# Projecting queries and keys of an attention kernel by Strassen's scheme: seven products of block sums in place of eight block products

## The chip, the cores and the metric

One Trainium2 chip, of which the kernel uses one core. The metric is the device time of one execution in microseconds (us), lower is better. Every time below comes from timed runs or from one profiled execution of the kernel. TensorE does the matrix products (PE in the profile; its weight loads, which overlap them, are PEld), VectorE is DVE, ScalarE is ACT, GpSimd is POOL, and SyncE, which issues most transfers, is SP.

## The reference

Two attentions over the same 2048 rows of 512 numbers, mixed by a gate. Side A is softmax attention of 32 heads over all 2048 keys. Side B is attention in four segments of 512 with a causal mask, plus a linear memory of the earlier segments.

```python
def _A_ref(x, wqkv, wo):
    qkv = (x @ wqkv).reshape(B, S, 3, H, Dh).transpose(2, 0, 3, 1, 4)
    q, k, v = qkv[0], qkv[1], qkv[2]
    p = softmax(einsum("bhqd,bhkd->bhqk", q, k) * Dh ** -0.5)
    return einsum("bhqk,bhkd->bhqd", p, v) ... @ wo
g = sigmoid((x * gate_w).sum(-1, keepdims=True))
return g * _A_ref(x, A_wqkv, A_wo) + (1 - g) * _B_ref(x, B_wq, B_wk, B_wv, B_wo, B_beta)
```

Here S = 2048, D = 512, H = 32, Dh = 16; all is float32. What the change touches is `x @ wqkv` for the queries and keys of side A.

## The kernel before

The rows of x are worked in four chunks of 512 (`CH`). Every matrix operand is split into a high half, rounded to the type float32r, and the low half that is left over; a product is then three products: high by low, low by high, high by high. So a tile of 128 outputs by 512 rows of x, with the 512 inputs in four steps of 128, is 12 matmuls.

The program has a projection stage, and a main loop behind it. In the projection stage first come the projections of side A ("all keys"): queries of chunks 0 and 1, keys and values of all four chunks. The queries of chunks 2 and 3 (`LATER`) are made in the main loop. Then come the projections of side B, its memory, and the first 96 steps of the search for the row maxima. The main loop does scores, exponentials, products with the values and the output projection.

The stage runs in slots. A slot (`slot`, L360) is 12 matmuls in four places of three; behind each place it calls whatever was posted there: `post(n, place, f)` counts from the current slot, `post_at` names the slot. Each engine executes in the order in which the code is written, so this decides what stands behind what in the queues.

A tile of queries or keys (`qk_tile`, L418) goes to a bank of `pr_ps` (two banks). A slot later ScalarE copies the bank to `full` (L433) and casts it to the high half `q1` (L434), VectorE subtracts for the low half `q2` (L441), and SyncE stores both (L430); `q1` and `q2` have three buffers each. Tiles of values (`v_tiles`, L470) are copied to `vs` by ScalarE (L481) and stored once for a chunk; `vs` has one buffer. Operands are loaded into raw buffers and split by ScalarE and VectorE (L403, L404). The first four tiles of queries (`first_tiles`, L456) are made side by side in four banks, so that the product can begin with the first 128 rows of the weights.

GpSimd writes, by twenty small transfers (L378), rows of ones into the tiles in which the main loop will hold keys (`kA`, `kB`), and makes minima for side B's feature map (L438). Other banks in the stage: `me_ps` (two, tag "me") and `me_sm` (four, tag "sm"), used by side B's memory and the maxima.

Of the kernel before, what the change touches and what calls it, by code (L numbers as in the profile page):

```python
# [19 lines left out]
D = 512  # L20
# [27 lines left out]
def gated_mix(ctx, tc, x, xT, wqkv, a_wo, b_wq, b_wk, b_wv, b_wo, beta, gate_w, out):  # L48
# [284 lines left out]
    with ExitStack() as p0:  # L333
# [15 lines left out]
        ones = wk1.tile([128, CH], F32, tag="dn", name="ones")[0:2]  # L349
# [10 lines left out]
        def slot(ps=None, l=None, r=None):  # L360

            terms = [(a, b, k) for k in range(KT) for a, b in ((1, 0), (0, 1), (0, 0))]
            for place in range(4):
                if ps is not None:
                    for n in range(3 * place, 3 * place + 3):
                        a, b, k = terms[n]
                        nc.tensor.matmul(ps, l(a, k), r(b, k), start=(n == 0), stop=(n == 11))  # L367
                for f in posted.pop((now[0], place), []):
                    f()
            now[0] += 1  # L370

# [4 lines left out]
        for i, t in enumerate(kbuf["A"] + kbuf["B"]):  # L376
            for r in range(2):
                post_at(6 + i, 1 + 2 * r, lambda t=t, r=r: nc.gpsimd.dma_start(  # L378
                    raw(t)[64 * r + 48:64 * r + 50], ones.unsqueeze(1).broadcast_to([2, 2, CH])))

        def halves(pool, tag, src, load_slot, split_slot, tiles=None, queue=nc.sync):
# [3 lines left out]
            def load(i):  # L385
                t = tiles[i] if tiles else None
# [11 lines left out]
            def split(k):  # L398
# [5 lines left out]
                nc.vector.tensor_sub(hold[1][:, k], w, hold[0][:, k].bitcast(F32))  # L404
# [13 lines left out]
        def qk_tile(side, w, xc, o, dst, then=None, ps=None, n0=0):  # L418

            if ps is None:  # L420
                ps = pr_ps.tile([128, CH], F32, tag="pr", name="pr")
                slot(ps, lambda a, k: w[a][:, k, o * 128:(o + 1) * 128], lambda b, k: xc[b][:, k, :])
# [5 lines left out]
            def store(i, t):  # L428
                to = dst[16 * i:16 * i + 16].rearrange("d h t -> (d h) t") if side == "A" else dst[i].rearrange("h d t -> (h d) t")
                nc.sync.dma_start(to, raw(t))  # L430
# [21 lines left out]
            post(n0, 0, e0)  # L452
            post(n0, 1, e1)
            post(n0 + 1, 1, e2)

        def first_tiles(w, xc):  # L456

            banks = [(pr_ps if o < 2 else me_ps).tile([128, CH], F32, tag="pr" if o < 2 else "me", name="pr") for o in range(NO)]
            for k in range(KT):
                for i, (a, b) in enumerate(((0, 0), (0, 1), (1, 0))):  # L460
# [3 lines left out]
                    for f in [f for place in ((0,), (1,), (2, 3))[i] for f in posted.pop((now[0], place), [])]:  # L464
                        f()
# [713 lines left out]
```

## Time and profile before

| what | value |
|---|---|
| median of 3 runs | 1751.49 us (1750.65 to 1752.21) |
| the profiled execution | 1749.92 us |
| its span, first to last instruction | 1748.2 us |
| granted TensorE clock, mean | 1.000 |
| projections of side A | 5.7 us to about 115 us |
| first score of the main loop | 284.69 us |

The page gives, for each engine, its busy time, share of the span and count of instructions, and then 40 equal slices of the span with the busy share of each in tenths. The chain of waits is followed back from the last instruction, at each step to what released it. A group row has line, engine, operation, output and inputs with shapes, count, then busy time and mean ns of one, and behind the second bar the engine's idle time just before these instructions with what ended it. A row of a timeline has start and duration in us. A merged row with "x2" lasts from the first start to the last end. In a table of stretches each engine's busy time is followed by its count; the last three numbers are the granted clock, the share in which the transfer engines were busy, and GB/s.

### The profile page before, as it was taken

The page shows a single profiled execution, that of the slowest core. Times are in us where ns is not written, and L with a number is a line of the kernel's source. Part 1 is how long each engine was busy: PE and PEld are TensorE (multiplying, and loading weights), DVE is VectorE, ACT ScalarE, POOL GpSimd, SP SyncE. Part 2 cuts the span into 40 slices and gives each one's busy share as a digit, 9 for nine tenths or more (in the row PEclk, how much of TensorE's full clock was granted, in tenths as well). Part 3 has the DMA queues.
Part 4 walks back from the last instruction along what each step waited for, and adds up shares of the span by engine and source line. Part 5 has one row for each costly group of instructions (what it writes and reads, how often), then busy time and mean ns, then how long its engine had stood idle before and what let it go on. Part 6 is the DMA issues. An engine that isn't in the chain of part 4 may idle for free.

```text
span 1748.2 us, 41466 instructions
## 1 busy us (share of the span) xinstructions
PE 1741.4 (100%) x15229; PEld 890.4 (51%) x15229; DVE 1558.4 (89%) x3283; ACT 1434.5 (82%) x2751; POOL 696.7 (40%) x954
## 2 busy tenths in 40 slices
PE   9999999999999999999999999999999999999999
PEld 7887775444444444444444444444444444444444
DVE  4337778999999999999999999999999999999931
ACT  5455556888889898888888888888888888888884
POOL 3012233324262427353534353444344353535443
PEclk9999999999999999999999999999999999999999
DMA  7677667435453446444545454444444444444542
GB/s 251 220 245 244 209 214 205 120 103 149 120 152 102 130 127 196 125 143 132 147 122 150 123 142 136 134 139 127 148 126 153 127 132 118 148 118 146 150 153 63
DMA packets 149115, 261.61 MB, mean 150 GB/s; under 512 B 38793, under 2 KB 61353, under 8 KB 148401
## 3 DMA queue, kind: packets, MB, share of 16 engines
q1 hardware_dynamic: 146464, 254.42, 48.8%
q0 software_dynamic: 2304, 4.29, 1.0%
q8 instruction: 121, 1.98, 0.5%
q14 instruction: 82, 0.66, 0.1%
q10 hardware_dynamic: 144, 0.26, 0.1%
HBM read 174.39 MB, written 83.25 MB: 147 GB/s over the span
## 4 chain that ended last, share of the span: by engine, by line
PE 99%; ACT 0%; DMA 0%; issue 0%; DVE 0%; ACTq 0%
PE ops L155 40%; PE st L815 27%; PE sm L242 14%; PE pr L367 13%; PE sm L155 2%; PE pr L462 1%; PE mt_ps L232 0%; PE tps L601 0%; PE sm L815 0%; DMA raw<-xT 0%; PE mps L615 0%; ACT p L838 0%; PE num L574 0%; PE den L578 0%; PE ops L1121 0%
## 5 line engine op out<-in xcount | busy, mean ns | idle before, releaser
L838 ACT ACTIVATE p<-st 128x512 f32<-128x512 f32 x2261 | 1190.9, 601 | 146.8 <-PE sm L242 93.5
L275 DVE TENSOR_REDUCE pm<-sm 128x1 f32<-128x512 f32 x2048 | 1276.1, 682 | 10.3 <-PE sm L242 8.9
L242 PE MATMUL sm<-kA,qA 48*128 48x512 f32 x2048 | 661.3, 424 | 0.0
L815 PE MATMUL st<-qA,kA 50*128 50x512 f32 x2014 | 656.3, 432 | 0.0
L155 PE MATMUL ops<-p,vA 128*17 128x256 f32 (+3 forms) x6360 | 552.7, 445 | 0.2 <-ACT p L838 0.2
L815 PEld LDWEIGHTS st<-qA,kA 50*128 50x128 f32 x2014 | 327.0, 185 | 423.0 <-ACT p L838 382.2
L242 PEld LDWEIGHTS sm<-kA,qA 48*128 48x128 f32 x2048 | 337.5, 185 | 11.4 <-DVE ph L450 4.6
L939 POOL TENSOR_TENSOR rcp<-rec,minus 128x32 f32<-128x32 f32 x43 | 234.8, 5461 | 82.9 <-DMA rec<-dend 76.9
L290 DVE CUSTOM_DVE_ANT_0 rest<-sm,mask 128x128 f32<-128x128 f32 (+3 forms) x512 | 246.4, 481 | 0.4 <-PE sm L242 0.4
L155 PEld LDWEIGHTS ops<-p,vA 128*17 128x17 f32 x6360 | 129.3, 96 | 214.8 <-issue 183.4
L819 POOL TENSOR_SCALAR_AFFINE_SELECT p<-p 128x512 f32<-128x512 f32 x128 | 79.4, 637 | 265.9 <-ACT p L838 261.4
L242 PE MATMUL sm<-kB,qB 48*128 48x128 f32 (+3 forms) x512 | 166.1, 385 | 0.0
L815 PE MATMUL st<-qB,kB 50*128 50x512 f32 (+1 forms) x495 | 105.5, 329 | 0.3 <-ACT mt L235 0.3
L441 DVE TENSOR_TENSOR q<-full,q 128x512 fp32r<-128x512 f32 x56 | 38.8, 694 | 74.1 <-ACT q L434 69.6
L815 PEld LDWEIGHTS st<-qB,kB 50*128 50x128 f32 x495 | 68.6, 186 | 62.1 <-ACT p L838 50.4
L155 PE MATMUL ops<-p,vB 128*17 128x128 f32 (+3 forms) x1504 | 88.3, 350 | 0.0
L242 PEld LDWEIGHTS sm<-kB,qB 48*128 48x128 f32 x512 | 80.0, 184 | 0.0
L214 POOL TENSOR_TENSOR dm<-pm 128x32 f32<-128x32 f32 x32 | 7.9, 247 | 165.6 <-DVE pm L275 165.6
L438 POOL TENSOR_SCALAR mn<-full 128x512 f32<-128x512 f32 x24 | 36.9, 1536 | 88.0 <-ACT full L433 88.0
L433 ACT COPY full<-pr 128x512 f32<-128x512 f32 x56 | 32.7, 584 | 37.9 <-PE pr L367 32.7
L223 POOL CAST ms<-pm 128x16 fp32r<-128x16 f32 x32 | 6.3, 196 | 126.5 <-DVE pm L290 126.4
L955 POOL TENSOR_TENSOR v<-v,inv 128x512 f32<-128x512 f32 x31 | 39.8, 1284 | 27.4 <-DMA inv<-rdA 23.6
(203 smaller groups left out, 1618.7 us busy)
## 6 DMA issues: line engine op xcount, KB each, us to landing
kA<-kdA SPq DMA_DIRECT2D x256, 128.0 KB
vA<-vdA SPq DMA_DIRECT2D x31, 544.0 KB
kA<-kdA SPq DMA_DIRECT2D x256, 64.0 KB
qB<-qdB SPq DMA_DIRECT2D x192, 64.0 KB
kB<-kdB SPq DMA_DIRECT2D x192, 64.0 KB
kdA<-q SPq DMA_DIRECT2D x32, 256.0 KB
qdB<-q SPq DMA_DIRECT2D x32, 256.0 KB
qA<-qdA SPq DMA_DIRECT2D x64, 128.0 KB
```

Source lines behind the costliest of these rows:

```text
L155: behind[0] = nc.tensor.matmul(*args, **kw)
L242: nc.tensor.matmul(ps[:, n0:n0 + n], rows(qt[u][:, :, s * 128:(s + 1) * 128], h, 48), rows(k[:, :, k0:k0 + n], h, 48), start=True, stop=True)
L275: nc.vector.tensor_reduce(pm[:, h, s, kc:kc + 1], ps, axis=AX.X, op=ALU.max, negate=True)
L290: nc.vector.tensor_tensor_reduce(out=tri["rest"][:, 0:w], in0=ps[:, n0:n0 + w], in1=tri["mask"][:, CH - w:], scale=-1.0, scalar=3.0e38, op ...
L367: nc.tensor.matmul(ps, l(a, k), r(b, k), start=(n == 0), stop=(n == 11))
L438: nc.gpsimd.tensor_scalar_min(ph["mn"], full, 0.0)
L441: nc.vector.tensor_sub(q2, full, q1.bitcast(F32))
L815: nc.tensor.matmul(ps[:, n0:n0 + CH - q0], rows(k[:, :, b * 128:(b + 1) * 128], h, 50), rows(q[:, :, q0:], h, 50), start=True, stop=True)
L819: nc.gpsimd.affine_select(out=x, in_=x, pattern=[[0, 4], [1, 128]], base=0, channel_multiplier=-1, compare_op=ALU.is_ge, fill=0.0)
L838: nc.scalar.activation(p[:, h], ps, AF.Exp, scale=SCALE)
L939: eng.tensor_tensor(r, rec, minus, op=ALU.pow)
L955: eng.tensor_mul(k["v"], k["v"], k["inv"])
```

## The change

Queries and keys of side A are now projected for two chunks at a time. Weights and the two chunks of x are cut into two by two blocks: 256 inputs, 256 outputs, and one chunk of 512 rows each. Strassen's scheme in Winograd's form makes the four output blocks from seven block products of sums of blocks; a block product is, for each of two tiles of 128 outputs, 6 matmuls of the old shape. A pair of chunks is thus 14 products of 6 matmuls (`pair_tiles`), with two products in a slot, and takes 7 slots. It is done three times: queries of chunks 0 and 1, keys of 0 and 1, keys of 2 and 3. Values stay plain; they come first (chunks 0 and 1) and between the two key pairs (chunks 2 and 3). The stage of side A has 37 slots in place of 40.

The sums of x (`s_sums`) are made once for a pair of chunks, in the raw buffers, and the sums of the weights (`t_sum`) as well; each sum is then split into halves like every operand. VectorE and GpSimd share these. The split sums lie in the key tiles of the main loop (`kbuf`) and in its query buffers, so the rows of ones are now written at slot 38 and later. The products' banks are read by VectorE: adds join the seven products (`sums`, `out_tile`), two with a sum kept in SBUF each, and an output tile is an add out of a bank into `full` where it was a copy by ScalarE. Low halves are subtracted by VectorE or, for half of the tiles of the first key pair, by GpSimd.

```diff
-        def slot(ps=None, l=None, r=None):
+        PARTS = (1, 0), (0, 1), (0, 0)
+        def slot(products=()):
...
+        def pair_tiles(w, ts, xs, ss, cs, dst, eng_):
+            steps, odd = [], [0]
+            for g in range(2):
...
+                def out_tile(o, c, ps, plus, eng, t=t):
+                    full = wk.tile([128, CH], F32, tag=("full", "am")[o // 2], name="full", bufs=2)
+                    nc.vector.tensor_add(full, ps, t[plus])
+                    q1 = wk.tile([128, CH], F32R, tag="q1", name="q1", bufs=3)
+                    q2 = wk.tile([128, CH], F32R, tag="q2", name="q2", bufs=3)
+                    nc.scalar.copy(q1, full)
...
+                    def low():
+                        eng.tensor_sub(q2, full, q1.bitcast(F32))
+                        store(1, q2)
+                    store(0, q1)
+                    post(*((1, 1) if odd[0] else (0, 3)), low)
...
+                    nc.scalar.copy(t["p1"], ps)
...
+                def sums(ps, g=g, t=t, out_tile=out_tile):
+                    for name, tag, bank, plus in (("u2", "ex", ps, "p1"), ("u3", "gw", t["p7"], "u2")):
+                        t[name] = wk1.tile([128, CH], F32, tag=tag, name=name)
+                        nc.vector.tensor_add(t[name], bank, t[plus])
+                    out_tile(2 + g, 1, t["p5"], "u3", nc.vector)
+                    nc.vector.tensor_add(t["u2"], t["p5"], t["u2"])
...
+                steps += [(quarter(0, 0), of_x(0, 0), "sm", first), (quarter(1, 0), of_x(0, 1), "sm", out(g, 0, "p1", nc.vector)),
+                          (of_t(0), of_s(0), "me", keep_bank("p5")), (of_t(2), of_s(2), "me", keep_bank("p7")),
+                          (of_t(1), of_s(1), "sm", sums), (of_t(3), of_x(1, 1), "sm", out(g, 1, "u3", eng_)),
+                          (quarter(1, 1), of_s(3), "sm", out(2 + g, 0, "u2", eng_))]
...
+                post(0, 1 + 2 * (m % 2), lambda: then(ps))
+                terms = [(l(a, k), r(b, k)) for k in range(2) for a, b in PARTS]
...
+            if not inner:
+                pss = [f() for f in banks]
+                for k in range(KT):
+                    slot([(pss[b], xs(p, k)[:, b * 128:(b + 1) * 128], w[q][:, k, :], k == 0 and n == 0, k == KT - 1 and n == 2)
+                          for n, (q, p) in enumerate(((0, 0), (1, 0), (0, 1))) for b in range(4)])
...
+        for k in range(KT):
+            nc.sync.dma_start(vraw[k], wv_[k * 128:(k + 1) * 128])
+            (nc.sync if k else nc.scalar).dma_start(xraw[0][k], xT[k * 128:(k + 1) * 128, 0:CH])
...
+        load_raw(xchunk(1), xraw[1])
+        load_raw(wq_, qraw)
...
+        def s_sums(x0, x1, engs):
+            for k, eng in engs:
+                eng.tensor_add(x1[2 + k], x1[k], x1[2 + k])
+                eng.tensor_sub(x1[k], x0[k], x1[k])
+                eng.tensor_sub(x0[k], x1[2 + k], x0[k])
+                eng.tensor_sub(x0[2 + k], x0[2 + k], x0[k])
...
+        post_at(1, 0, lambda: s_sums(xraw[0], xraw[1], ((0, V), (1, P))))
+        for k in range(KT):
+            post_at(4, 2, lambda k=k: w_split(wAq, qraw, k))
+        for i, eng in ((0, (V, P)), (2, (V, P)), (1, (V, P)), (3, (V, P))):
+            post_at(4, 2, lambda i=i, eng=eng: t_sum(i, qraw, eng))
+        for n, i in enumerate((0, 2, 1, 3)):
+            post_at(4 + n, 3, lambda i=i: s_split(i, xraw[0], xraw[1]))
+            post_at(4 + n, 3, lambda i=i: t_split(tqs, i, qraw, (V, P)))
...
+            post_at(7, 2 * i, lambda i=i: load_k_raw(i))
+        for k in range(KT):
+            post_at(10, k, lambda k=k: w_split(wAk, kraw, k))
+        for n, (i, eng) in enumerate(((0, (V, P)), (2, (V, P)), (1, (V, P)), (3, (V, P)))):
+            post_at(10, 3, lambda i=i, eng=eng: t_sum(i, kraw, eng))
+            post_at(11 + n // 2, 1 + 2 * (n % 2), lambda i=i: t_split(tks, i, kraw, (V, P)))
...
+        for c, i, n in ((2, 0, 11), (2, 1, 14), (3, 0, 15), (3, 1, 15)):
+            post_at(n, 0, lambda c=c, i=i: load_x(c, i, (c, i) == (3, 1)))
...
-                post_at(6 + i, 1 + 2 * r, lambda t=t, r=r: nc.gpsimd.dma_start(
+                post_at(38 + i, 1 + 2 * r, lambda t=t, r=r: nc.gpsimd.dma_start(
...
-            for o in range(NO if 0 < c and c not in LATER else 0):
-                qk_tile("A", wAq, xc, o, qd["A", o, c])
-            for o in range(NO):
-                qk_tile("A", wAk, xc, o, kd["A", o, c])
-            v_tiles("A", wAv, xc, c)
+        v_tiles("A", wAv, flat(xs[0]), 0, inner=False, banks_=[sm_bank] * 4)
+        v_tiles("A", wAv, flat(xs[1]), 1, behind_=1, banks_=[me_bank, me_bank, pr_bank, pr_bank])
+        pair_tiles(wAq, tqs, [flat(xs[0]), flat(xs[1])], ss, (0, 1), {(o, c): qd["A", o, c] for o in range(NO) for c in range(NCH)}, V)
+        pair_tiles(wAk, tks, [flat(xs[0]), flat(xs[1])], ss, (0, 1), dk, P)
+        wBq = halves(wp, "wq", b_wq, 28, 30, [None, two], queue=nc.gpsimd)
+        v_tiles("A", wAv, lambda a, k: xs[2](a, k), 2, banks_=[sm_bank] * 4)
+        v_tiles("A", wAv, lambda a, k: xs[3](a, k), 3, behind_=1, banks_=[me_bank, me_bank, pr_bank, pr_bank])
+        pair_tiles(wAk, tks, [lambda a, k: xs[2](a, k), lambda a, k: xs[3](a, k)], ss, (2, 3), dk, V)
```

Where instructions stand now. TensorE, the end of a tile of keys and the begin of one of values before, with weights `wk`, `wv` and x in halves h and l, and bank numbers behind `pr`:

```order
L367 MATMUL pr_458<-xh_263,wkl_323 128x512
L367 MATMUL pr_458<-xl_264,wkh_322 128x512
L367 MATMUL pr_458<-xh_263,wkh_322 128x512
L367 MATMUL pr_483<-wvh_372,xl_264 128x512
L367 MATMUL pr_483<-wvl_373,xh_263 128x512
L367 MATMUL pr_483<-wvh_372,xh_263 128x512
```

The end of the second product of the query pair now, in slot 8, and the begin of the third in slot 9; `kA0`, `kA1` hold a sum of x in halves, `tq` a sum of the query weights:

```order
L366 MATMUL pair_490<-xh_277,wql_274 128x512
L366 MATMUL pair_490<-xl_278,wqh_273 128x512
L366 MATMUL pair_490<-xh_277,wqh_273 128x512
L366 MATMUL pair_520<-kA0_192,tq_299 128x512
L366 MATMUL pair_520<-kA1_193,tq_297 128x512
L366 MATMUL pair_520<-kA0_192,tq_297 128x512
```

A tile that was four rounds of three matmuls is now two rounds, with sums as operands in some of them.

VectorE, in the slots of chunk 0's keys before (`q` are the halves of output tiles):

```order
L441 TENSOR_TENSOR q_399<-full,q_398 128x512
L404 TENSOR_TENSOR wvl<-ph,wvh 128x512
L441 TENSOR_TENSOR q_434<-full,q_433 128x512
L441 TENSOR_TENSOR q_457<-full,q_456 128x512
L404 TENSOR_TENSOR xl<-raw,xh 128x512
L441 TENSOR_TENSOR q_480<-full,q_479 128x512
```

And from slot 10 of the query pair now (`u` and `p` are sums kept in SBUF, `pair` a bank, `raw` the key weights, `tk` and `kB` the halves of their sums):

```order
L574 TENSOR_TENSOR wkl<-raw,wkh 128x256 x2
L498 TENSOR_TENSOR u_550<-pair,p_506 128x512
L498 TENSOR_TENSOR u_552<-pair,u_550 128x512
L474 TENSOR_TENSOR full<-pair,u_552 128x512
L500 TENSOR_TENSOR u_550<-pair,u_550 128x512
L574 TENSOR_TENSOR wkl<-raw,wkh 128x512 x2
L638 TENSOR_TENSOR raw<-raw 128x256 x4
L474 TENSOR_TENSOR full<-pair,u_552 128x512
L483 TENSOR_TENSOR q_557<-full,q_556 128x512
L574 TENSOR_TENSOR kB_200<-raw,tk 128x256
```

Between two reads of a bank there now stand six instructions on the key weights.

GpSimd, some of its early work in the stage before:

```order
L472 MEMSET vs 128x128
L517 DMA gh<-beta 16x4x1 x8
L378 DMA kA_194<-ones 2x2x512 x2
L378 DMA kA_195<-ones 2x2x512 x2
L378 DMA kA_196<-ones 2x2x512 x2
```

And now (`ph`, `am` and `raw` hold x and the query weights, in which the sums are made):

```order
L621 TENSOR_TENSOR ph<-raw,ph 128x512
L622 TENSOR_TENSOR raw<-raw 128x512
L623 TENSOR_TENSOR raw<-ph,raw 128x512
L624 TENSOR_TENSOR raw<-raw 128x512
L638 TENSOR_TENSOR ph<-ph 128x256
L638 TENSOR_TENSOR ph<-am,ph 128x256
L638 TENSOR_TENSOR am<-am,ph 128x256
L638 TENSOR_TENSOR am<-am 128x256
L574 TENSOR_TENSOR tq<-ph,tq 128x256 x2
L534 MEMSET vs 128x128
L574 TENSOR_TENSOR tq<-am,tq 128x256 x2
```

Sums and splits stand where small transfers stood; those follow at slot 38 and later.

246 lines of the change are left out of this document (169 added, 77 removed).

## The prediction

> **What bounds the kernel now.** I read the page first, for the engine that sets the end, then the chain of waits in order of time, for the part that the change rewrites, and then busy time by stretches.
>
> ```profile
> span 1748.2 us, 41466 instructions
> PE 1741.4 (100%) x15229; PEld 890.4 (51%) x15229; DVE 1558.4 (89%) x3283; ACT 1434.5 (82%) x2751; POOL 696.7 (40%) x954
> ...
> DVE  4337778999999999999999999999999999999931
> ...
> PEclk9999999999999999999999999999999999999999
> ...
> PE 99%; ACT 0%; DMA 0%; issue 0%; DVE 0%; ACTq 0%
> ```
>
> The chain that ended last is TensorE for 99% of the span, at the full granted clock. So TensorE's work counts one for one, and other engines count only where they make it wait. VectorE has room in the first four slices (4, 3, 3, 7 tenths) and none after the seventh. The change works in the first three. The chain in order of time shows that stretch:
>
> ```profile
> 5.72 11.14 PE pr L462 x48
> 16.87 130.99 PE pr L367 x576
> ```
>
> 48 matmuls in 11.14 us, then 576 in 130.99 us without one break: 0.2274 us each, whatever the two operands are. The projections for all keys are the first 480 of these 624: 11.14 + 432 x 0.2274 = 109.4 us, to about 115.1 us. Twelve matmuls, one slot of the program, are 2.73 us.
>
> ```profile
> core 0: us, PE busy (x) PEld busy (x) DVE busy (x) ACT busy (x) POOL busy (x), PEclk, DMA share, GB/s
> 0.00:5.72 5.72, 3.83 (x20) 3.67 (x21) 1.36 (x6) 1.90 (x2) 3.64 (x13) 1.00 0.57 182
> 5.72:16.87 11.15, 11.14 (x49) 8.91 (x49) 8.24 (x13) 7.14 (x13) 0.00 (x0) 1.00 1.00 346
> 16.87:27.77 10.90, 10.90 (x47) 8.85 (x48) 5.34 (x9) 9.35 (x17) 7.77 (x16) 1.00 0.71 258
> 38.70:49.60 10.90, 10.90 (x50) 9.03 (x49) 2.08 (x3) 4.21 (x7) 0.32 (x1) 1.00 0.59 209
> ```
>
> In this stage VectorE is busy 2 to 8 us of 11, ScalarE 4 to 9, GpSimd nearly idle after the start. This idle time pays for the change's additions.
>
> **What it removes.** Three pairs of chunks (queries 0 and 1, keys 0 and 1, keys 2 and 3) go from 96 matmuls each to 14 products of 6, that is 84. All have the old shape, 128x128 against 512 columns, so I price them at the old pitch: 36 x 0.2274 = **8.2 us** less, 37 slots where there were 40. Values keep their 192 matmuls. What follows is placed relative to the first slot of the B side, so it moves up whole.
>
> **What it adds at the very start.** The values now go first, and each round's second group of four multiplies the low half of the weights, not of x.
>
> ```profile
> 5.61 0.69 DVE L508 TENSOR_TENSOR xl<-raw,xh 128x512 fp32r<-128x512 f32 x1
> 5.72 1.16 PE L462 MATMUL pr<-xh,wqh 128*128 128x512 f32 x4 [0.47 <-DVE xh L506]
> 6.22 0.68 DVE L508 TENSOR_TENSOR wql<-raw,wqh 128x512 fp32r<-128x512 f32 x1
> ```
>
> VectorE still makes x's low half first and the weights' second, which is there at 6.90; the first four matmuls are issued by 5.72 + 4 x 0.2274 = 6.63. I add **0.3 us**. Later rounds have the operands about a round ahead.
>
> **What it adds on VectorE and GpSimd.** The durations:
>
> ```profile
> L275 DVE TENSOR_REDUCE pm<-sm 128x1 f32<-128x512 f32 x2048 | 1276.1, 682 | 10.3 <-PE sm L242 8.9
> L955 POOL TENSOR_TENSOR v<-v,inv 128x512 f32<-128x512 f32 x31 | 39.8, 1284 | 27.4 <-DMA inv<-rdA 23.6
> L441 DVE TENSOR_TENSOR q<-full,q 128x512 fp32r<-128x512 f32 x27 | 18.6, 692 | 65.0 <-ACT q L434 60.7 <-DMA qdA<-q 3.2 <-ACT full L433 1.0
> 12.02 1.29 DVE L404 TENSOR_TENSOR wkl<-raw,wkh 128x512 fp32r<-128x512 f32 x2 [0.80 <-ACT wkh L403]
> 11.37 1.14 ACT L403 CAST wkh<-raw 128x512 fp32r<-128x512 f32 x2 [0.87 <-DMA raw<-wqkv]
> 1738.22 0.42 DVE L964 TENSOR_TENSOR hl<-v,hl 128x256 fp32r<-128x256 f32 x1
> 1715.46 0.25 POOL L942 TENSOR_TENSOR rec<-rcp,err 128x32 f32<-128x32 f32 x1
> ```
>
> A 512-column VectorE instruction takes 0.69 us, and two in a row 1.29, so in a full queue each costs 0.60. The new adds read PSUM, which no 512-column add does here; a reduction that reads PSUM takes 0.682, so I price them alike. A 256-column one takes 0.42, or 0.34 in a row (0.42 less the same 0.09). GpSimd takes 1.28 us at 512 and 0.25 at 32 columns, so by the line between them 0.73 at 256. ScalarE's casts cost 0.57 in a row.
>
> Up to slot 4: 12 splits and 4 sums of x, 16 x 0.60 = 9.6 us on VectorE and 4 x 1.28 = 5.1 on GpSimd, done by slot 5. Slots 4 to 7, where the operands of the query products are made: on VectorE 2 + 8 instructions of 512 columns (weight splits, splits of the x sums) and 2 + 4 + 4 of 256 (weight splits, weight sums and their splits): 10 x 0.60 + 10 x 0.34 = 9.4 us; on GpSimd 8 x 0.73 = 5.8. Slots 8 to 14, the query products: 14 adds out of PSUM and 8 low halves, 22 x 0.60 = 13.2; and the key weights' splits and sums, 2 x 0.60 + 10 x 0.34 = 4.6; on GpSimd 5.8 again. So VectorE has 27.2 us to do between the middle of slot 4 and the end of slot 14, 10.5 slots or 28.7 us. It fits, by 1.5 us, if GpSimd does not hold it up. Slots 15 to 21: 14 adds, 4 low halves and 4 splits of x, 13.2 of 19.1 us. Slots 30 to 36: 14 adds, 8 low halves, 4 splits, 15.6 of 19.1. ScalarE (0.57, and 0.31 at 256 columns by the same subtraction as VectorE's) has in slots 4 to 7 six evictions, 10 casts of 512 and 10 of 256 columns, 12.2 us of 10.9, and in slots 8 to 14 2 + 2 evictions, 8 + 2 casts and 10 small ones, 11.1 of 19.1: it runs some 1.5 us late into slot 8, ahead of every use.
>
> What is late next if VectorE is late: a product's bank comes free when an add has read it, and the four "sm" banks come round every four such products, about 5.5 us. Up to that a late add costs TensorE nothing. In slot 10 the key weights' splits and sums stand ahead of the add that frees that slot's second bank, so the slack is used from there to slot 16.
>
> Does GpSimd hold VectorE up? The trace has a few overlaps, of GpSimd's one-input minimum with VectorE's two-input work:
>
> ```profile
> 187.55 1.98 POOL L438 TENSOR_SCALAR mn<-full 128x512 f32<-128x512 f32 x1 [1.29 <-ACT full L433]
> 229.05 1.49 POOL L438 TENSOR_SCALAR mn<-full 128x512 f32<-128x512 f32 x1 [17.88 <-ACT full L433]
> 187.49 0.69 DVE L530 SCALAR_TENSOR_TENSOR jk<-xg,gw 128x512 f32<-128x512 f32 x1 [1.49 <-DMA dend<-dn]
> 188.10 1.09 DVE L450 SCALAR_TENSOR_TENSOR ph<-full,ex 128x512 f32<-128x512 f32 x1
> 229.58 0.69 DVE L441 TENSOR_TENSOR q<-full,q 128x512 fp32r<-128x512 f32 x1 [0.82 <-ACT q L434]
> ```
>
> At 187.5 GpSimd grows by 0.49 us beside one VectorE instruction, and the next VectorE instruction by 0.40; at 229.6 VectorE starts 0.53 us into GpSimd's instruction and loses nothing. So the two exclude each other for about 0.41 us of GpSimd's one-input instruction. A two-input one reads twice as much: 0.82 of 1.28 us, 64%. Bounds: nothing, and the whole instruction. With 64% VectorE's 27.2 us become 27.2 + 0.64 x 11.6 = 34.6, which is 5.9 over; the ring of banks takes 5.5, so 0.4 us of stall. The budget leaves out that a low half also waits for its cast:
>
> ```profile
> 144.08 0.69 DVE L441 TENSOR_TENSOR q<-full,q 128x512 fp32r<-128x512 f32 x1 [0.37 <-ACT q L434]
> ```
>
> 0.37 us, for some 12 low halves that no other work stands in front of, is 4.4 us, and I let 1.3 of it come through. I take **1.7 us** in all; the bounds are 0 and, with whole instructions, 27.2 + 11.6 - 28.7 - 5.5 + 1.3 = 5.9.
>
> [...]
>
> **Transfers.** At the start x's chunk 1 and the query weights are now queued behind the first 2.1 MB at once, 4.2 MB in all. By the two first rows of the stretches 182 x 5.72 + 346 x 11.15 = 4.9 MB are there at 16.87, where slot 4 first uses chunk 1. The key weights are loaded at slot 7, when the x sums' splits have left their buffers, and used at slot 10, 8 us later, 3 us of transfer at 346 GB/s; eight tiny loads of GpSimd's (beta) stand at slot 8 as they did. All of it is hidden; a late weight would stop ScalarE's queue, and with it every eviction.
>
> Per pair of products the same 16 stores of 0.262 MB go out in 19.1 us, which had 32.8 us for a chunk with queries. In slots 8 to 21 there are 32 of them (8.4 MB), a store of values (1.1), the key weights (1.05) and chunks 2 and 3 (2.1): 12.7 MB in 38.2 us, 331 GB/s. The transfers of the first 60 us before, in 40 slices of 1.5 us:
>
> ```profile
> GB/s 0 96 285 392 395 275 302 377 305 343 400 335 209 164 328 192 166 371 394 287 213 261 290 130 82 3 0 311 351 345 90 335 59 135 287 270 147 206 382 403
> ```
>
> And the waits of the first 126 us that a store ended (total, times, longest):
>
> ```profile
> DVE q L441 <- DMA qdA<-q: 3.2, 2, 3.0
> ACT q L434 <- DMA qdA<-q: 1.1, 2, 0.9
> ```
>
> Slices moved up to 403 GB/s, and a full stretch of 11 us 346, so there is room, but little. The high and low halves keep three buffers each; when four query tiles came out within two slots, VectorE waited for a store once 3.0 us long. The products' tiles come three in two slots at the closest. I add **0.5 us**, bounds 0 and 3. Twenty small DMA issues of GpSimd and the gate's weights move to slots 38 to 47, beside its minima of 1.49 us; 2 x 0.57 + 1.49 = 2.6 of 2.73 us a slot in three slots (issue 0.57, from the row below). Their results are used more than a slot later, so nothing; without that cover a few tenths.
>
> ```profile
> L378 POOL DMA_DIRECT2D kA<-ones x16 | 9.1, 573 | 2.2 <-DVE ones L350 1.3 <-DMA kA<-ones 0.7
> ```
>
> **Sum.** -8.2 + 0.3 + 1.7 + 0.5 = **-5.7 us**. The profiled execution took 1749.92 us, 1.7 more than its span and 1.6 less than the median of the three runs, 1751.49. From the profiled one the forecast is 1744.2, from the median **1745.8 us**, which I take.
>
> **Rivals.** *Everything hides* (chance 0.20): GpSimd's half runs between VectorE's adds, which read PSUM and have one SBUF input, and no store is waited for. Then -8.2 + 0.3 = -7.9: 1743.6. For it speaks VectorE's 1.5 us of room; against it, the stretched 1.09.
>
> *Whole instructions exclude each other* (0.16): each GpSimd add blocks VectorE for its 1.28 or 0.73 us. Then the stall is 5.9 us, and with 0.3 and 0.5 the gain is 1.5: 1750.0, no change. For it, the 0.49 and 0.40 at 187.5; against it, 229.58.
>
> *The transfers become the bound, and the kernel is slower* (0.14): in slots 8 to 21 the three buffers of high halves wait for stores, ScalarE's next cast stands behind them, the adds' buffers fill and the banks stay taken. It is decided by the rate: 12.7 MB in 38.2 + 7.9 us is 275 GB/s; below that the whole gain is gone. At the 258 GB/s of 16.87 to 27.77 it would take 49.2 us, 11.0 more, and -7.9 + 11.0 = +3.1: 1754.6. For it, that row and the 3.0 us wait; against it, that the DMA share was 0.71 there, so not at its limit, and 346 with the share at 1.00.
>
> That the change does not do what it says is excluded: TensorE's order has 36 matmuls fewer.
>
> **Chances and range.** The forecast has 0.50, with a range of its own of 1743 to 1748.5. A measurement of this kernel can tell about 0.2%, 3.5 us, from no change. Faster by more: 0.45 of the forecast's and 0.20, together 0.65. Within: 0.05 and the 0.16, 0.21. Slower by more: most of the last rival, 0.14. The range that leaves 2 in 10 out runs from 1742.5, the full gain with the runs' spread of 0.8 us under it, to 1753, into the last rival.
>
> **What would show it.** Right: the chain stays TensorE to 99%; 444 projection matmuls before the B side's first, which starts near 115.1 - 5.7 = 109.4 us; TensorE waits for VectorE only in slots 9 to 16, some 2 us in all; the low-half wait at the start near 6.9 us. Each rival has its mark: no waits at all and a start near 107.2; GpSimd and VectorE rows stretched to their summed durations, TensorE waiting 6 us for the x sums' splits and for banks; or ScalarE and VectorE waiting for stores of queries with the DMA share at 1.00. It is wrong if the main loop, 284.7 us to the end, changes its length by more than a microsecond, since nothing in it is touched.

## The result, and the profile after

The changed kernel took 1755.96 us, median of 8 runs (1754.84 to 1757.33), beside 1750.63 us for the kernel before, also 8 (1749.91 to 1752.21): ratio 1.003, 95% interval 1.0019 to 1.0041. It is slower by 5.3 us; 1745.8 was predicted. From the page after, in the order of the page before:

```profile
span 1753.9 us, 41539 instructions
PE 1738.8 (99%) x15193; PEld 883.1 (50%) x15193; DVE 1612.7 (92%) x3361; ACT 1435.1 (82%) x2765; POOL 732.3 (42%) x984
...
DVE  8677778999999999999999999999999999999931
...
PEclk9999999999999999999999999999999999999999
...
PE 93%; DMA 1%; ACT 1%; issue 1%; POOL 0%; DVE 0%; DVEq 0%; POOLq 0%; ACTq 0%
```

36 matmuls are gone (15229 to 15193), and TensorE's share of the chain fell from 99% to 93%: it waits. The first score in the chain in order of time:

```profile
290.50 0.49 PE st L1013
```

Before it stood at 284.69, so all 5.8 us are lost ahead of it. From there to the end 1463.4 us pass; before, 1463.5. With the 8.2 us saved it should have come at 276.5, so 14.0 us were lost. Below, a wait's length is the time from the start of one matmul to the start of the next, less the 0.2274 us that it takes without a wait. The largest, in TensorE's timeline (start, duration, engine, line, operation, count, and in brackets the idle time with what ended it):

```profile
5.98 1.84 PE L366 MATMUL pair<-wvh,xh 128*128 128x512 f32 x4
7.66 1.08 PE L366 MATMUL pair<-wvl,xh 128*128 128x512 f32 x4
...
45.01 1.65 PE L366 MATMUL pair<-kA,tq 128*128 128x512 f32 x6 [1.35 <-DVE full L474]
47.63 0.50 PE L366 MATMUL pair<-xh,tq 128*128 128x512 f32 x1 [0.97 <-DVE full L474]
47.97 0.40 PE L366 MATMUL pair<-xl,tq 128*128 128x512 f32 x1
...
53.84 0.50 PE L366 MATMUL pair<-xh,wkl 128*128 128x512 f32 x1 [1.01 <-DVE u L498]
...
71.33 0.50 PE L366 MATMUL pair<-kA,wkl 128*128 128x512 f32 x1 [0.37 <-ACT p L490]
...
75.29 0.50 PE L366 MATMUL pair<-wvh,x 128*128 128x512 f32 x1 [0.97 <-DVE x L574]
...
123.85 0.50 PE L366 MATMUL pr<-xh,wql 128*128 128x512 f32 x1 [1.58 <-ACT full L430]
128.49 0.50 PE L366 MATMUL pr<-xh,wql 128*128 128x512 f32 x1 [1.58 <-ACT full L430]
```

They form four groups: the start (0.9 us: the first matmul comes 0.26 later than before, and the first eight take 0.68 more), 45 to 62 us (4.4, for VectorE's reads of banks), 62 to 90 us (3.4: the end of the key products of chunks 0 and 1, and the values of chunk 2, whose x is split late), and the first tiles of side B (3.8, for ScalarE). After each wait the second matmul comes after 0.34 us instead of 0.23 (47.63 to 47.97); with 14 waits that is 1.5 more. The sum is 14.0.

In those first eight TensorE does not wait: the first four matmuls come 0.56, 0.43 and 0.43 us apart with no idle time between them, about twice the pitch. The trace's records of the granted clock begin, at full speed, only at 7.45 us here; in the kernel before they begin at 4.25, ahead of its first product.

Why VectorE is late, in its timeline and GpSimd's:

```profile
13.89 1.66 POOL L621 TENSOR_TENSOR ph<-raw,ph 128x512 f32<-128x512 f32 x1 [3.10 <-DVE xl L574]
14.44 1.67 DVE L622 TENSOR_TENSOR raw<-raw 128x512 f32<-128x512 f32 x1
15.63 1.62 POOL L622 TENSOR_TENSOR raw<-raw 128x512 f32<-128x512 f32 x1
16.13 1.66 DVE L623 TENSOR_TENSOR raw<-ph,raw 128x512 f32<-128x512 f32 x1
...
26.47 1.82 DVE L574 TENSOR_TENSOR kA<-ph,kA 128x512 fp32r<-128x512 f32 x2
32.73 1.28 DVE L574 TENSOR_TENSOR kA<-raw,kA 128x512 fp32r<-128x512 f32 x2
34.26 0.68 DVE L474 TENSOR_TENSOR full<-pair,p 128x512 f32<-128x512 f32 x1
...
40.51 1.29 DVE L574 TENSOR_TENSOR wkl<-raw,wkh 128x512 fp32r<-128x512 f32 x2 [0.61 <-ACT wkh L573]
41.72 2.63 DVE L638 TENSOR_TENSOR raw<-raw 128x256 f32<-128x256 f32 x4
44.27 0.68 DVE L474 TENSOR_TENSOR full<-pair,u 128x512 f32<-128x512 f32 x1
```

The sums of x go in step, one VectorE instruction every 1.69 us, where they come every 0.72 us without GpSimd (e2, from 14.12 us); 26.47 and 32.73 are the same work beside GpSimd and without it. The first output add ends the backlog at 34.26, and it takes the 0.68 that were priced. From 39.9 the key weights keep VectorE for 4.4 us; behind them, at 44.27, stands the add that TensorE waits for.

And the stores, in the timelines of ScalarE, GpSimd and VectorE, and by stretches:

```profile
70.17 0.62 ACT L477 CAST q<-full 128x512 fp32r<-128x512 f32 x1 [3.03 <-DMA kdA<-q]
...
109.83 3.39 POOL L403 TENSOR_TENSOR xl<-raw,xh 128x512 fp32r<-128x512 f32 x2 [2.16 <-ACT xh L402]
115.20 1.46 POOL L393 DMA_DIRECT2D raw<-b_wv  x2
...
126.29 0.62 ACT L431 CAST q<-full 128x512 fp32r<-128x512 f32 x1 [2.50 <-DMA kdA<-q]
...
128.12 0.69 DVE L438 TENSOR_TENSOR q<-full,q 128x512 fp32r<-128x512 f32 x1 [2.41 <-DMA kdA<-q]
```

```profile
60.00:70.00 10.00, 9.82 (x44) 7.79 (x43) 5.07 (x8) 1.79 (x3) 0.41 (x1) 1.00 0.99 325
...
120.00:125.00 5.00, 3.42 (x15) 2.49 (x15) 2.43 (x4) 2.24 (x4) 2.78 (x5) 1.00 1.00 379
125.00:130.00 5.00, 3.42 (x16) 2.47 (x15) 2.59 (x5) 2.64 (x5) 2.76 (x6) 1.00 1.05 401
```

A cast waits until the store of three tiles ago has left its buffer, with the transfer engines fully busy. The B value weights are issued only at 115.20, behind GpSimd's low halves of x.

### The profile page after: what moved, and what is told of

It is laid out like the page before. It is cut to its first block, busy times and chain, and to the rows that moved or that the text cites. A ratio compares the mean times of both kernels' runs of the same rounds, so it can differ in the third digit from the quotient of the medians.

```text
span 1753.9 us, 41539 instructions
## 1 busy us (share of the span) xinstructions
PE 1738.8 (99%) x15193; PEld 883.1 (50%) x15193; DVE 1612.7 (92%) x3361; ACT 1435.1 (82%) x2765; POOL 732.3 (42%) x984
## 4 chain that ended last, share of the span: by engine, by line
PE 93%; DMA 1%; ACT 1%; issue 1%; POOL 0%; DVE 0%; DVEq 0%; POOLq 0%; ACTq 0%
PE ops L155 40%; PE st L1013 28%; PE sm L242 14%; PE pr L366 8%; PE sm L155 2%; PE pair L366 0%; DMA raw<-b_wv 0%; PE mt_ps L232 0%; PE tps L799 0%; PE sm L1013 0%; POOL xl L403 0%; DMA kA<-ones 0%; PE mps L813 0%; PE num L772 0%; PE den L776 0%
## 5 line engine op out<-in xcount | busy, mean ns | idle before, releaser
L1153 POOL TENSOR_TENSOR v<-v,inv 128x512 f32<-128x512 f32 x31 | 39.9, 1286 | 27.9 <-DMA inv<-rdA 24.4
L477 ACT CAST q<-full 128x512 fp32r<-128x512 f32 x24 | 14.9, 621 | 44.5 <-DVE full L474 29.5
L155 PEld LDWEIGHTS ops<-p,vB 128*17 128x17 f32 x1504 | 33.9, 96 | 30.2 <-issue 25.7
```

The costliest lines, as they stand in the source:

```text
L155: behind[0] = nc.tensor.matmul(*args, **kw)
L477: nc.scalar.copy(q1, full)
L1153: eng.tensor_mul(k["v"], k["v"], k["inv"])
```

## Experiments

Each run beside the kernel before on the same chip (1750.2 to 1751.0 us). The last five columns are from one profile each: what the first eight matmuls take beyond 8 x 0.2274 us (0.10 in the kernel before), TensorE's waits of over 0.25 us in three stretches, and how long the granted clock was at half speed after the start and ahead of the end, all in us.

| run | median, us | ratio, 95% | start | 39 to 62 | 62 to 90 | 100 to 150 | half clock |
|---|---|---|---|---|---|---|---|
| the change | 1755.96 | 1.0019 to 1.0041 | 0.78 | 4.4 | 3.4 | 3.8 | 0 |
| e1 no GpSimd sums | 1753.74 | 1.0010 to 1.0029 | 0.44 | 2.4 | 3.5 | 4.3 | 3.4 |
| e2 all on VectorE | 1758.02 | 1.0030 to 1.0063 | 0.17 | 4.0 | 3.3 | 4.9 | 3.4 |
| e3 no key-weight work | 1751.38 | 0.9995 to 1.0014 | 0.45 | 0 | 3.1 | 4.1 | 0 |
| e4 order of values | 1754.6, one run | | 0.68 | 4.7 | 2.9 | 3.8 | 0 |
| e5 ring of four | 1757.09 | 1.0022 to 1.0048 | 0.44 | 4.6 | 0.4 | 6.8 | 6.8 |
| e6 x by GpSimd's queue | 1756.2 | 1.0018 to 1.0041 | 0.47 | 4.8 | 2.4 | 4.1 | 6.8 |
| e7 key weights later | 1755.66 | 1.0016 to 1.0036 | 0.45 | 6.3 | 0.4 | 4.4 | 3.4 |
| e8 B's loads spread | 1759.82 | 1.0036 to 1.0061 | 0.45 | 4.3 | 3.2 | 5.3 | 3.4 |
| e9 key weights on GpSimd | 1751.27 | 0.9998 to 1.0015 | 0.45 | 2.5 | 1.9 | 3.2 | 0 |
| e10 ring of four, clean | 1753.41 | 1.0006 to 1.0024 | 0.44 | 4.5 | 0.9 | 3.9 | 0 |
| e11 no B weight transfer | 1756.64, one run | | 0.45 | 4.7 | 3.2 | 4.1 | 3.4 |
| e12 together | 1752.35 | 1.0002 to 1.0019 | 0.47 | 2.1 | 1.9 | 2.3 | 3.4 |
| e13 more banks for B | 1754.06 | 1.0012 to 1.0030 | 0.45 | 4.5 | 3.6 | 2.8 | 0 |
| e14 together, keys earlier | 1751.81 | 0.9999 to 1.0016 | 0.45 | 2.3 | 0 | 4.1 | 3.4 |
| e15 same, B lows on GpSimd | 1748.61 | 0.9982 to 0.9999 | 0.45 | 2.1 | 0 | 2.7 | 0 |
| **e16 B's weights earlier** | **1745.70** | **0.9963 to 0.9984** | 0.66 | 0.8 | 0.8 | 0 | 0 |
| e17 e16 without that | 1747.22 | 0.9973 to 0.9990 | 0.54 | 0.9 | 0.9 | 1.4 | 0 |

**VectorE's backlog (e1 to e4, e7, e9).** e1 skips GpSimd's sums and fills its low halves with zeros.

```diff
             for k, eng in engs:
+                if eng is P:
+                    continue
```

> Left out: GpSimd's part of the sums of x and of the weights is not done, and GpSimd's low halves of the weight sums are filled with zeros (an instruction that only writes). Theory 1, exclusion (GpSimd's two-input instructions and VectorE's block each other for most of their length, which makes VectorE late in slots 1 to 14): VectorE's sums of x take 0.69 us instead of 1.67, its splits of the sums 0.61 each, the first output add comes at about 31 us instead of 34.3, and TensorE's waits from 45 to 55 us (4.5 us in the changed kernel) fall under 1 us; the time falls by 3 to 5 us, to about 1752. Theory 2, transfers (stores stand behind loads, and the rings of three make the engines wait): VectorE's instructions get shorter but the waits stay, the time falls by less than 1.5 us. Both expect the waits at 123 to 132 us to stay, since the low halves of x for side B are still GpSimd's.

Its first output add, in VectorE's timeline, has to wait for TensorE:

```profile
31.04 0.69 DVE L474 TENSOR_TENSOR full<-pair,p 128x512 f32<-128x512 f32 x1 [1.88 <-PE pair L366]
```

So running beside GpSimd cost VectorE 3.2 us by then (34.26), and about half of the waits at 45 to 62 us. e2 gives GpSimd's two-input work to VectorE.

```diff
-        post_at(1, 0, lambda: s_sums(xraw[0], xraw[1], ((0, V), (1, P))))
+        post_at(1, 0, lambda: s_sums(xraw[0], xraw[1], ((0, V), (1, V))))
```

> Nothing left out: all sums, splits and low halves of the side A stage and of chunk 0 for side B go to VectorE; GpSimd keeps fills and transfers. Theory 1, exclusion: VectorE alone does the sums of x in 4.9 us, where both together took 5.8, and the weight sums in 2.7 against 3.5, so TensorE's waits in slots 9 to 16 shrink by 2 to 4 us; GpSimd also issues the side B weight loads about 6 us earlier, so the waits at 123 to 132 us shrink too; the time falls by 4 to 8 us, to 1748 to 1752. Rival, VectorE's throughput is the limit: with 16 us more work in slots 1 to 33 the waits grow by 3 us or more, to 1759.

2 us slower than the change, but not for lack of time by the first output add: it comes at 31.36, 2.9 us earlier than with the work shared, and the waits at 45 to 62 us are not longer (4.0 against 4.4). What is longer is the start of side B, whose low halves of x VectorE now makes too (4.9, with 1.5 at 115 us for one of its adds), and 3.4 us at half clock. Up to the first output add, sharing gained nothing. e3 leaves out the splits and sums of the key weights; GpSimd fills their tiles with zeros.

```diff
-            post_at(10, k, lambda k=k: w_split(wAk, kraw, k))
+            pass
```

> Left out: the splits and sums of the key weights in slots 10 to 12; their tiles are filled with zeros by GpSimd. The loads stay. Theory 3, order (this work stands in VectorE's and ScalarE's queues ahead of the adds that free the banks): the waits from 45 to 55 us vanish, 4 us or more less, although VectorE still reaches its first output add at 34.3 us. Theory 1 alone: VectorE is 3 us late before that work begins, and some 2 us of the waits stay. Theory 2: all waits stay.

No wait is left at 45 to 62 us, though its first output add stands at 34.09, as late as in the change. The contention alone is hidden by the banks; it takes the key weights behind it. e4 swaps the second and third group in the first round of values.

```diff
-                          for n, (q, p) in enumerate(((0, 0), (1, 0), (0, 1))) for b in range(4)])
+                          for n, (q, p) in enumerate(((0, 0), (0, 1), (1, 0))) for b in range(4)])
```

> The first values: in each round the group with the low half of x comes before the group with the low half of the weights. If the wait at the start is VectorE's order (x's low half is made first), the 0.77 us gap before the second group falls to about 0.4, and the values of chunk 1 start at about 17.3 us instead of 17.66. If it is the later landing of the weights, the gap stays.

The start still loses 0.7, but the clock came up as late here (7.15 us), so this run says nothing about the order. The other runs do. In the seven whose clock is full only after 6.0 us (the change, e4, e5, e14 to e17) the first two matmuls are 0.42 to 0.57 us apart, in the kernel before and the other eleven 0.30 to 0.34. In ten of these eleven the second group of four waits 0.2 us for the weights' low half, and the first eight matmuls take 0.35 us more than in the kernel before. e7 spreads the key-weight work over slots 11 to 15.

```diff
-            post_at(10, k, lambda k=k: w_split(wAk, kraw, k))
+            post_at(11 + (k > 1) + (k > 2), (2, 3, 2, 0)[k], lambda k=k: w_split(wAk, kraw, k))
...
-            post_at(10, 3, lambda i=i, eng=eng: t_sum(i, kraw, eng))
+            post_at(13, 1, lambda i=i, eng=eng: t_sum(i, kraw, eng))
```

> The splits and sums of the key weights stand in slots 11 to 15 instead of 10 to 12, spread between the bank reads, and the loads of x that reuse their buffers move with them (slot 16). If the 4.5 us that TensorE waits at 45 to 55 us are a matter of order (key-weight work ahead of bank reads in VectorE's and ScalarE's queues), they fall to 1 us or less and the total to about 1752.5. If VectorE and GpSimd simply have too much to do by then, the same 4 to 5 us appear later, in slots 14 to 17, and the total stays at 1755 to 1757.

The waits only moved, to 51 to 62 us (6.3): 2.9 for a read of a bank by VectorE, 3.5 for the operands themselves. Order alone does not help while VectorE has this work to do. e9 gives most of it to GpSimd, which is busy for 7.9 of the 26 us from 36 to 62 us in the change.

```diff
-        for n, (i, eng) in enumerate(((0, (V, P)), (2, (V, P)), (1, (V, P)), (3, (V, P)))):
+        for n, (i, eng) in enumerate(((0, (P, P)), (2, (P, P)), (1, (P, P)), (3, (P, P)))):
```

> All sums of the key weights, all low halves of these sums and the low halves of the first two rows of weights are made by GpSimd instead of VectorE, one slot later; x's loads for chunks 2 and 3 and the tiny loads of beta move behind them. Nothing is left out. If the 4.5 us at 45 to 55 us are VectorE's queue holding key-weight work ahead of bank reads, they go as they went with that work left out (to below 1 us), and the total is 1751 to 1752.5. If two-input work on GpSimd blocks VectorE for its whole length wherever it stands, the wait stays at 3 us or more there or in slots 15 to 18 (49 to 60 us), total 1755 to 1757.

0.8 us of waits for VectorE are left; the other 1.8 are for GpSimd's last low halves, which come late. 4.7 us are gained with nothing left out.

**The rings of halves (e5, e6, e10).** e5 gives every fourth tile two other buffers.

```diff
+                    if ntile[0] % 4 == 0:
+                        q1 = wk1.tile([128, CH], F32R, tag="dn", name="q1")
+                        q2 = wk1.tile([128, CH], F32R, tag="ones", name="q2")
```

> Every fourth product tile takes its high and low halves from two other buffers, so that the ring of halves waiting for their stores is four deep instead of three; nothing else changes. If the waits of the key products of chunks 0 and 1 (slots 15 to 21, 3.4 us at TensorE) come from casts and subtractions that wait for a store to free their buffer, most of that goes (2 to 3 us, total 1753 to 1754), and the waits before slot 15 (4.5 us) stay. If the waits come from VectorE's and ScalarE's load, or the stores are late by more than a buffer's turn, nothing changes within 0.5 us (1755 to 1756). The waits of the first B tiles (3.8 us) use the ring of three as before and stay in both.

The waits at 62 to 90 us fell to 0.4, but the edit made a new one. VectorE's timeline shows it, and the stretch behind it:

```profile
128.10 0.48 DVE L720 MEMSET ones<- 2x512 f32 x1 [8.81 <-DMA kdA<-q]
```

```profile
130.00:135.00 5.00, 4.54 (x11) 3.58 (x12) 5.00 (x9) 3.68 (x7) 5.00 (x11) 0.50 0.79 247
```

The tile of ones, moved into the ring's buffer, waited for the last store and held VectorE. e10 makes it on GpSimd and later (`nc.gpsimd.memset` at slot 43, and `% 4 == 1`).

> The ring of halves four deep again, but the tile of ones, which had shared the ring's last buffer and held VectorE for 8.8 us, is made by GpSimd six slots after the products. If the store rings are what delays slots 15 to 25, the 3.4 us there go and the wait of the first B tiles is no longer than before (3 to 4 us): total 1752.5 to 1754. If the lost time only moves on to wherever the transfers are next at their limit, the B tiles' wait grows to 6 us or more and the total stays at 1755.5 to 1757.

0.9 us are left at 62 to 90, the B side keeps its 3.9, and 2.5 us are gained. e6 issues x's loads for chunks 2 and 3 from GpSimd.

```diff
-            load_raw(xchunk(c)[256 * i:256 * i + 256], t)
+            load_raw(xchunk(c)[256 * i:256 * i + 256], t, nc.gpsimd)
```

> The loads of x for chunks 2 and 3 are issued by GpSimd's queue instead of SyncE's; nothing else changes. If the stores of halves are late because they stand behind these loads in SyncE's queue (issue at 56 to 63 us), the waits of the key products of chunks 0 and 1 shrink from 3.4 us to about 1 (total near 1753.5). If they are late because the transfers themselves share the rate, the waits stay at 3 us or more (1755 to 1756), and loads behind GpSimd's own subtractions may come later and add to it.

2.4 us stay, in one wait at 65.87, and 3.4 us of half clock follow it. The stores came no earlier: VectorE waited 4.66 us for one at 64.5 us, where in the change it waited 2.61 at 62.5. The loads ahead of the stores in SyncE's queue are not the cause.

**The start of side B (e8, e11, e13).** e8 puts the low halves of B's first x on VectorE and the last weights' loads later.

```diff
-        xc = halves(xp, "x", xchunk(0), 28, 32, eng=P)
+        xc = halves(xp, "x", xchunk(0), 28, 32)
...
-        wBk = halves(wp, "wk", b_wk, 36, 40, [None, two], queue=nc.gpsimd)
+        wBk = halves(wp, "wk", b_wk, 39, 42, [None, two], queue=nc.gpsimd)
```

> The low halves of the B side's first chunk go back to VectorE, so that the loads of the value weights no longer stand behind them in GpSimd's queue, and the loads of the last weights are issued three slots later, their splits two. If the 3.8 us that TensorE waits at 123 to 132 us come from one late burst of 2.1 MB that delays the stores, the waits fall below 1 us and the total to about 1752. If they come from the work of the first B tiles itself, they stay (1755 to 1756); if VectorE has no room for the low halves, the wait appears in slots 30 to 36 instead (at 103 to 122 us).

Worse: VectorE had no room (a new wait of 0.87 us at 115 us), and a wait of 1.87 us for an eviction by ScalarE came up at 144 us. Part of its time is not the edit's: in its profile the clock was halved from 46.2 to 49.6 us, ahead of it. e11 fills the B value and key weights with zeros instead of loading them.

```diff
+                    if tag in ("wv", "wk"):
+                        nc.gpsimd.memset(t, 0.0)
```

> The B side's value and key weights (2.1 MB) are not transferred: their tiles are filled with zeros by GpSimd at the place where the loads were issued. So B's values and keys are wrong, and the transfers of 115 to 130 us are 2.1 MB lighter. If the burst of these loads delays the stores for which the first B tiles wait, the 3.8 us at 123 to 132 us fall below 1 us. If the stores of the last eight products alone are too many, or VectorE is late, 2 us or more stay.

At 123 to 132 us 1.35 of the 3.8 are left, but a wait of 2.4 us came up at 142 us. ScalarE's timeline there:

```profile
141.28 0.62 ACT L408 CAST xh<-raw 128x512 fp32r<-128x512 f32 x1 [5.90 <-DMA raw<-xT]
141.80 0.58 ACT L541 COPY vs<-pr 128x512 f32<-128x512 f32 x1
```

It stood 5.9 us for the next chunk of x, and an eviction behind it. The burst matters, but is not all, and time won ahead of a late load is lost at it. e13 gives two B tiles of queries and two of values other banks.

```diff
-                qk_tile(wBq, xc, o, qd["B", o, c], pqs.append if c else None)
+                qk_tile(wBq, xc, o, qd["B", o, c], pqs.append if c else None, None if c or o < 2 else me_bank)
```

> The third and fourth tile of the B side's first queries, and of its first values, use two other PSUM banks, so that four tiles instead of two may wait for ScalarE; nothing else changes. If the 3.8 us at 123 to 132 us are VectorE's and ScalarE's backlog of the last products meeting a ring of two banks, they fall below 1 us and the total is 1752 to 1753. If ScalarE's wait for stores is longer than four tiles (11 us), 2 us or more stay.

The wait for the two banks went, and 2.2 us for the low halves of B's value weights took its place (129.7 and 132.1 us).

**Together (e12, e14 to e17).** e12 is e9, e10 and e8, with half of the B key weights loaded at slot 30.

> Nothing left out: key-weight sums and low halves on GpSimd (as in e9), the ring of halves four deep (as in e10), the low halves of B's first chunk on VectorE with the last weights' loads three slots later (as in e8), and half of those weights loaded at slot 30 into buffers that are free by then. If the three causes add up as their waits did (4.5, 3.4 and 3.8 us), at most 3 us of waits are left and the total is 1744 to 1747, faster than before. If the transfers bound the whole stage, the waits come together again before the B side and the total stays above 1752.

The waits fell by more than 5 us, yet only 3.6 us were gained. TensorE's timeline after its last wait, and that stretch:

```profile
119.83 0.50 PE L365 MATMUL pr<-xh,wql 128*128 128x512 f32 x1 [2.10 <-ACT full L429]
...
121.22 0.63 PE L365 MATMUL pr<-xl,wqh 128*128 128x512 f32 x1
121.64 0.63 PE L365 MATMUL pr<-xh,wqh 128*128 128x512 f32 x1
```

```profile
120.00:125.00 5.00, 5.00 (x16) 3.91 (x17) 1.99 (x4) 3.58 (x7) 3.93 (x7) 0.66 0.86 258
```

The granted clock fell: 0.42 us from matmul to matmul instead of 0.23, and 16 recorded in 5 us where 22 would fit. e14 begins the keys a slot earlier and adds e13; e15 is e14 without e8's part and the load at slot 30.

```diff
+            post_at(*((10, 0), (10, 0), (11, 2), (12, 0))[k], lambda k=k: w_split(wAk, kraw, k, P if k < 2 else V))
+        for i, s, p, s2, p2 in ((0, 10, 1, 12, 2), (2, 10, 1, 13, 0), (1, 13, 0, 14, 0), (3, 13, 0, 14, 2)):
```

> As e12, with the key weights' work on GpSimd begun one slot earlier, x's chunk 2 split from slot 17 on instead of 19, and the B side's first tiles on four banks. Nothing is left out. Theory (three causes, each with its own wait, and a lowered clock after a wait of TensorE of over 2 us): waits of 1 to 2 us are left beside the start, no lowered clock, total 1744 to 1747. Rival (VectorE or the transfers bound the stage whatever the order): waits of 5 us or more again, total 1749 to 1752.

> As e14, but the B side's first low halves of x on GpSimd and its weight loads as in the change. If only VectorE's backlog and the number of banks matter at the start of the B side, the total is within 1 us of e14, or lower, since VectorE has 2.4 us less to do. If the late burst of weight loads matters too, 1 to 3 us of waits for stores come back there.

e14 met the clock again (0.54 to 0.78 at 127.5 to 132.5 us, after 2.27 us). e15 is 3.2 us better. Two things differ, and no run parts them: the loads went back to where they had stood, and VectorE no longer makes the low halves of the B side's x. The waits show the second: 1.5 us at 108.8 and 0.4 at 101.7 for VectorE's adds are gone, while those for the B value weights stay (2.3 in both). e14's 3.4 us of half clock are gone too. e16 puts all key sums ahead of the low halves on GpSimd, gives the first B query tile the fourth buffer, and loads B's weights between the low halves of x and before; e17 leaves out the last.

```diff
+                post_at(31 if tag == "wv" else load_slot, 2, lambda: load(0))
+                post_at(33 if tag == "wv" else 30 if tag == "wk" else load_slot, 1 if tag == "wv" else 3, lambda: load(1))
```

> As e15, and: the key weights' four splits stand together in slot 10 and all their sums ahead of the low halves on GpSimd; the B value weights are loaded at slots 31 and 33 instead of 34, between the low halves of x, and half of the B key weights at slot 30; the first B query tile uses the fourth buffer too. Nothing is left out. Theory (each wait has the cause named): the waits of 2.1 us at 54 us (GpSimd's low halves of key-weight sums late) and of 2.3 us at 122 to 125 us (low halves of B's value weights late behind a wait for stores) shrink to below 0.7 us each, total 1745 to 1747. Rival (the transfers around the B side's start keep them late wherever the loads stand): only the first goes, total 1747 to 1749.

> As e16 with the B weights' loads where the change has them. Theory: the wait at 54 us is gone and the 2.3 us at 122 to 125 us stay, total 1746.5 to 1748.5, 1 to 2 us over e16. Rival: no difference from e16 within 0.5 us.

e16 beats both kernels: 1745.70 us against 1750.29, ratio 0.9973 (0.9963 to 0.9984). Its page, its first score in the chain, and its GpSimd in place of the rows at 115:

```profile
span 1743.4 us, 41552 instructions
...
PE 96%; DVE 1%; DMA 1%; ACT 1%; issue 0%; SPq 0%; POOL 0%; DVEq 0%; ACTq 0%; POOLq 0%
```

```profile
279.32 0.49 PE st L1027
```

```profile
96.69 0.71 POOL L392 DMA_DIRECT2D raw<-b_wv  x1 [4.62 <-DVE wql L402]
...
106.74 0.73 POOL L392 DMA_DIRECT2D raw<-b_wv  x1
```

The two loads stand 18.5 and about 9 us earlier. On the B side no wait over 0.25 us is left that the kernel before does not have (six of 0.3 us, from 171 us on here), and the first score comes 5.4 us before the old one.

## Why the prediction was wrong

**The 8.2 us of matmuls** were right: 36 fewer, and in the change (-8.2 + 14.0 = 5.8, as the first score shows) and in e16 (-8.2 + 2.8 = -5.4) the sum closes. So were the price of an add out of PSUM (0.68) and that the main loop keeps its length. What failed is what was added to it, 2.5 us where 14.0 were lost. Side B's first matmul was forecast at 109.4 us and came at 116.66; the rest was lost behind it.

**The stall of 1.7 us** (VectorE and GpSimd) was 4.4. The mechanism was as told: a backlog from slots 4 to 8, then the key weights in slot 10 ahead of an add. Two sizes were off. "64%" of a GpSimd instruction as exclusive was taken from one-input rows; two-input ones go in step, 1.69 us for both, which leaves 0.97 to 1.09 of GpSimd's 1.28 to it alone (VectorE's part being 0.72 or 0.60), 76 to 85%. With that the prediction's own sum gives 3.1 to 4.2 in place of 1.7, an estimate, and the rival of whole instructions was nearer with its 5.9. And VectorE's waits for ScalarE's casts, let through with 1.3, recur at the splits of the key-weight sums (0.39, 1.04 and 1.04 us at 45.95, 48.61 and 52.16), since the two engines take turns there.

**"I add 0.5 us" for transfers** failed too: 3.4 us at 62 to 90, of which a ring of four leaves 0.9 (e10). The rival of transfers said that rings of three would wait, which they did, and gave 1754.6. That this is near the measured time is luck: it charged 11.0 us to the rate of the transfers alone. It was to decide at 275 GB/s, and at 60 to 70 us 325 were moved with the share at 0.99. A mean rate says nothing of whether the store three tiles back has landed.

**"It moves up whole"**, said of all that follows, was the step with no term at all: 3.8 us. The products' adds end later than copies did, so VectorE and ScalarE reach side B with a backlog and two banks; the low halves of its x had gone to GpSimd, and the weights' loads behind them. e11, e13 and e16 against e17 each show a part of this; their shares can't be added, since each wait covers the next.

**The start**, 0.3, was 0.9, but not for a wait. Where the clock was up in time the first eight matmuls lose 0.35 us (ten runs), so the 0.3 was right; in the change's profile the clock came up late instead (records from 7.45 us). **The restarts**, 1.5 us, had no term. The chance of 0.14 for slower was too low: the sum priced each edit on an idle engine and the bounds left out what stands behind it.

## What to carry to other kernels

When work leaves the bottleneck engine for engines that share its queues, follow each added instruction to what stands behind it up to the next stage that feeds the bottleneck, and look at ring depths, not mean rates. Removing one wait tends to expose the next (e5, e11, e13), so judge a mechanism by the waits in its own place and the version by the sum. Put added work on the engine that is idle at that time (e9); halving work between VectorE and GpSimd at the same time won nothing up to the first output add (e2). Issue the next stage's loads ahead of work that waits.

## What the runs showed of the hardware

The granted clock is 1.00 or 0.50 in the traces' records, and it changes only at steps of 3.41 us, whose phase differs from run to run (one begins at 7.45 us in the change, at 4.25 in the kernel before). Two such steps of e12, and two of e10, with TensorE's busy time first:

```profile
117.01:120.42 3.41, 1.31 (x7) 0.76 (x6) 2.96 (x5) 2.84 (x6) 2.36 (x5) 1.00 0.76 226
120.42:123.83 3.41, 3.41 (x10) 2.64 (x9) 1.90 (x3) 1.99 (x5) 3.41 (x7) 0.50 0.78 216
...
120.49:123.90 3.41, 2.23 (x10) 1.50 (x8) 0.00 (x0) 0.49 (x1) 1.96 (x4) 1.00 1.03 410
123.90:127.31 3.41, 1.71 (x7) 1.42 (x8) 2.14 (x4) 3.21 (x7) 2.97 (x6) 1.00 1.06 398
```

In e12 a wait of 2.3 us fell into one step, which left TensorE idle for 2.10 of 3.41 us, and the next step ran at half clock. In e10 a wait of 3.04 us fell across two steps (1.18 and 1.70 idle), and the clock stayed. In all 19 profiles every step at full clock in which TensorE was idle for 1.90 us or more was followed by one at half clock, and none with 1.87 or less. Half clock for 3.41 us costs 1.7 us more than the wait, an estimate from these rows (3.41 x 0.50). A wait of 2.1 us meets it or not by its place: estimated from the steps, in half of the executions, (2.1 + 3.41 - 2 x 1.90) / 3.41.
